# Four instead of eight second-layer value tiles of the first batch element before the next element's values

## The chip, the cores and the metric

The kernel runs on one core of one Trainium2 chip. The metric is the device time in microseconds of one execution, the median over several. A NeuronCore has a matrix engine (TensorE, here PE, with its weight loads as PEld), a vector engine (VectorE, DVE), a scalar engine (ScalarE, ACT), GpSimd (POOL) and SyncE (SP). In this kernel SP issues every transfer between the chip's main memory and the core's on-chip memory; 16 DMA engines carry the bytes out. Each engine executes its own instructions in order and waits for the others by semaphores.

## What is computed

Two layers of a decoder run for one new token of each of four batch elements. A layer is an attention block and a feed-forward block, each behind a layer norm and with a residual addition. Both layers have the same weights and read the same key and value caches. Cut to what matters, the reference is:

```python
x = A_x                                             # 4 x 1 x 512
for layer in range(2):
    h = layernorm(x)
    q = (h @ wq).reshape(B, 1, 32, 128)             # 32 query heads, 8 key/value heads
    p = softmax(q @ k_cache.T * 128 ** -0.5)        # 4096 positions, 4 query heads share a cache head
    x = x + (p @ v_cache).reshape(B, 1, 4096) @ wo
    h = layernorm(x)
    x = x + (gelu(h @ w_gate) * (h @ w_up)) @ w_down
```

The caches are in bfloat16, 4 elements x 8 heads x 4096 positions x 128: 33.5 MB of keys and as much of values. The second layer's attention of an element needs the first layer's complete result for that element, and nothing of the other elements.

## The kernel before

**Tiles.** The eight cache heads are two groups of four (`GH = 4`). Each head's cache is two tiles of 512 KB (`NT = 2`, 128 partitions x 16 positions x 128), so an element has 16 key tiles and 16 value tiles. The key tiles have 16 fixed buffers (`KT`), enough for one element. Value tiles go through seven buffers (`KV_BUFS = 7`).

**Order over elements.** Call the first and second layer's attention of element b F(b) and S(b). Keys are loaded once per element: they are transposed in place on DVE (`Keys.turn`, line 372), used for F(b), and stay until S(b) has used them; only then may the next element's keys overwrite them. Values are too large to stay, so they are loaded twice, once for F(b), once for S(b). Two tiles of element 0 (`KEEP = 2`) are kept from F(0) for S(0) and are loaded once. A value tile below is named by its use: F1-0 to F1-15 are the tiles of F(1) in order of use, S0-0 to S0-15 those of S(0).

One stage, `attend(b2, b1)`, does the scores of S(b2), lets the keys of element b1 into the key buffers as these become free, turns them, and does F(b1). Then `dense` does the feed-forward block of element b1's first layer, and behind it come the second layer's queries for element b1, after which the next stage can free the key buffers. All the work of S(b2) on values that is not done early in the stage is a filler: `dense` and the lines after it call `fill(n)`, which is `Values.step` of S(b2), at ten places with ten tiles in all, and the next stage calls `rest` for what is left.

**The planned order of values.** One list, `order` (lines 441 to 446), fixes the sequence of all value tiles: F(0), then for each b the first `early[b]` tiles of S(b), all of F(b+1), and the remaining tiles of S(b). `early` is eight for element 0 (`TG`, one head group) and four for the others (`2 * NT`, one head pair). Both loads (`load_v`) and uses (`Values.step`) follow this list, and an assertion holds the uses to it. `load_v` issues the next load as soon as one of the seven buffers is free. A tile's buffer is free once its 16 matmuls (line 481, `ot`) are done. While `seen["hold"]` is set, only second-layer tiles may be loaded.

**Keys against values on SP's queue.** In a stage, four key loads (line 365) follow each of the four score blocks of S(b2), as each block frees four key tiles. For element 0 the last four are left out there and issued after the first four tiles of S(0) were used:

```python
if not (t and early[b2] == TG):          # lines 519 and 520
    keys.load(GH)
...
vals2.step(2 * NT)                        # lines 534 to 538
if early[b2] == TG:
    keys.load(GH)
    seen["hold"] = False
    load_v()
```

In the other stages `hold` is taken off right after the score blocks (lines 521 to 523). The rest of the early tiles of S(b2) is used while keys turn: `early - 5` tiles after the first block of F(b1)'s scores (line 560), and the last one after the softmax of that group has begun (line 566). With `early` of four both of these are empty.

Of the kernel before, what the change touches and what calls it, by code (L numbers as in the profile page):

```python
# [30 lines left out]
def kernel(  # L31
# [14 lines left out]
    B, Sq, D = A_x.shape  # L46
# [9 lines left out]
    NT = C // CH  # L56
# [5 lines left out]
    TG = GH * NT  # L62
# [373 lines left out]
    def value_order(b, last):  # L436
        if not last:
            return [(b, last, g, s, t) for g in groups(b) for s in range(GH) for t in range(NT)]
        return [(b, last, g, s, t) for g in groups(b + 1) for s in (3, 2, 0, 1) for t in range(NT)]

    early = [TG] + [2 * NT] * (B - 2)
    order = value_order(0, 0)
    for b in range(B - 1):
        n = early[b]
# [300 lines left out]
```

## Time and profile before

| | |
|---|---|
| median of 6 runs | 317.67 us (316.12 to 318.26) |
| the profiled execution's own time | 318.18 us |
| its span, first to last instruction | 316.4 us |
| PE, DVE, ACT busy | 213.2, 171.1, 28.9 us |
| bytes read | 113.5 MB, 359 GB/s over the span |
| DMA queue's packets, share of 16 engines' span | 93.8% |
| value loads | 118 into value buffers, 8 into freed key buffers at the end, 512 KB each |
| key loads | 64 of 512 KB |

The profile gives, for one execution, the busy time of each engine, the granted clock of PE, the bytes that the DMA engines moved in each slice or in a chosen window, the order in time of each engine's instructions with the wait before each, and the chain of work that ended last, traced back from the end. "SPq" is the issue of a transfer by SP; its landing is the arrival of the last byte. A busy DMA engine isn't always one at its best rate, so the GB/s of a window says more than the busy share. "Turn" below is the DVE transposition of a key tile, 1214 ns each on the mean.

### The profile page before, as it was taken

To read this page: it belongs to the slowest core of one execution; us is meant where nothing else is said; L and a number is where in the kernel's file an instruction comes from. 1 tells how busy PE (TensorE), PEld (TensorE's weight loads), DVE (VectorE), ACT (ScalarE), POOL (GpSimd) and SP (SyncE) were. 2 spreads that over 40 slices of the span, in tenths; PEclk is the share of its full clock that TensorE was granted. 3 is DMA by queue.
4 is the path that set the end of the run, shared out by engine and by line. 5 is a ranking of instruction groups with operands and counts; after the bars stand their busy time and mean duration, and the time that the engine had idled before them with its cause. 6 is when DMAs were issued, how large, how long until landed. Compare 5 with 4: busy or idle time off the path is not lost.

```text
span 316.4 us, 8713 instructions
## 1 busy us (share of the span) xinstructions
PE 213.2 (67%) x3844; PEld 122.3 (39%) x3844; DVE 171.1 (54%) x481; ACT 28.9 (9%) x70; POOL 0.7 (0%) x6
## 2 busy tenths in 40 slices
PE   1460585343576826989876589899762897998875
PEld 0010244121324314556342246564411464645654
DVE  5575751013248875525469874453789543545133
ACT  0002001000002020300020204000202040003100
POOL 0000000000000000000000000000000000000000
PEclk9999999999999555555595555575855555759555
DMA  7999999999939999999999999999999999999900
GB/s 256 383 411 388 409 410 404 351 376 388 390 125 356 404 395 410 407 407 390 356 314 411 410 407 393 355 404 407 408 409 409 408 374 339 407 367 409 368 9 3
DMA packets 35526, 114.09 MB, mean 361 GB/s; under 512 B 3224, under 2 KB 9120, under 8 KB 35488
## 3 DMA queue, kind: packets, MB, share of 16 engines
q1 hardware_dynamic: 35488, 113.53, 93.8%
q8 instruction: 30, 0.49, 0.6%
q14 instruction: 8, 0.07, 0.1%
HBM read 113.51 MB, written 0.00 MB: 359 GB/s over the span
## 4 chain that ended last, share of the span: by engine, by line
DMA 50%; PE 23%; DVE 13%; SPq 9%; issue 3%; ACT 1%; DVEq 0%; ACTq 0%
DMA v<-in_A_v_cache_dram 26%; DMA kt<-in_A_k_cache_dram 21%; PE ot L481 6%; PE sc L383 5%; DVE kt L372 4%; DMA wd_sb<-in_B_w_down_dram 3%; SPq L127 3%; PE rows L280 3%; SPq L133 3%; PE rows L314 3%; PE y L347 2%; PE rows L225 2%; PE x L429 1%; DVE pp L410 1%; SPq L128 1%
## 5 line engine op out<-in xcount | busy, mean ns | idle before, releaser
L481 PEld LDWEIGHTS <-v 128*128 128x128 bf16 x1920 | 59.3, 104 | 52.8 <-DMA v<-in_A_v_cache_dram 30.8
L481 PE MATMUL ot<-pe,v 128*128 128x4 bf16 x1920 | 63.2, 166 | 22.3 <-DMA v<-in_A_v_cache_dram 21.0
L372 DVE STREAM_TRANSPOSE kt<-kt 128x1024 f32<-128x1024 f32 x64 | 74.7, 1214 | 4.8 <-DMA kt<-in_A_k_cache_dram 4.8
L383 PE MATMUL sc<-kt,qb 128*32 128x512 bf16 x512 | 64.2, 557 | 15.8 <-DVE kt L372 11.2
L215 DVE STREAM_TRANSPOSE rows<-rows 128x512 f32<-128x512 f32 (+1 forms) x23 | 16.3, 707 | 39.4 <-PE rows L225 20.0
L383 PEld LDWEIGHTS <-qb 128*32 128x32 bf16 x512 | 17.7, 117 | 45.6 <-issue 33.8
L402 ACT ACTIVATE pp<-sc,nm 128x512 bf16<-128x512 f32 x16 | 11.0, 688 | 155.5 <-DVE junk L398 155.4
L489 DVE TENSOR_TENSOR OT_bf<-ot,rden 128x8 bf16<-128x8 f32 (+1 forms) x40 | 6.5, 163 | 34.0 <-PE ot L481 33.5
L429 PE MATMUL x<-pp,ident_bf 128*32 128x128 bf16 x256 | 9.1, 283 | 20.7 <-DVE pp L410 20.6
L280 PE MATMUL rows<-wo_sb,OT_bf 128*1 128x512 bf16 (+1 forms) x136 | 17.2, 611 | 7.3 <-DMA wo_sb<-in_A_wo_dram 6.3
L225 PE MATMUL rows<-wq_sb,xn_bf 128*1 128x512 bf16 (+1 forms) x160 | 18.9, 623 | 4.7 <-DMA wq_sb<-in_A_wq_dram 4.4
L389 DVE TENSOR_REDUCE m<-sc 128x1 f32<-128x512 f32 x16 | 10.8, 675 | 12.5 <-PE sc L383 12.5
L429 PEld LDWEIGHTS <-ident_bf 128*32 128x32 bf16 x256 | 6.6, 121 | 26.4 <-issue 24.6
L410 DVE STREAM_TRANSPOSE pp<-pp 128x512 bf16<-128x512 bf16 x16 | 11.3, 704 | 5.7 <-ACT pp L402 5.4
L432 ACT CAST pe<-x 128x512 bf16<-128x512 f32 x16 | 9.4, 585 | 21.0 <-PE x L429 21.0
L347 PE MATMUL y<-H_bf,wd_sb 128*128 128x1 bf16 (+1 forms) x280 | 8.4, 165 | 3.8 <-DMA wd_sb<-in_B_w_down_dram 3.0
L249 DVE TENSOR_TENSOR qb<-qe,amask 128x256 bf16<-128x256 f32 x16 | 6.8, 425 | 6.2 <-PE qe L246 6.2
L347 PEld LDWEIGHTS <-wd_sb 128*128 128x128 bf16 x280 | 7.9, 101 | 5.2 <-DMA wd_sb<-in_B_w_down_dram 4.0
L225 PEld LDWEIGHTS <-xn_bf 128*1 128x1 bf16 (+1 forms) x160 | 4.6, 111 | 12.8 <-issue 11.5
L246 PE MATMUL qe<-qm,t_bf 128*128 128x64 bf16 x16 | 3.5, 216 | 8.8 <-DVE qm L236 6.7
L415 PE MATMUL den<-zx,mean_f 128*128 128x16 f32 x32 | 8.9, 357 | 0.0
L420 DVE RECIPROCAL rden<-den 128x16 f32<-128x16 f32 x16 | 4.0, 251 | 8.5 <-PE den L415 8.0
(78 smaller groups left out, 124.3 us busy)
## 6 DMA issues: line engine op xcount, KB each, us to landing
v<-in_A_v_cache_dram SPq DMA_DIRECT2D x118, 512.0 KB, 8.7
kt<-in_A_k_cache_dram SPq DMA_DIRECT2D x64, 512.0 KB, 10.4
wq_sb<-in_A_wq_dram SPq DMA_DIRECT2D x2, 2048.0 KB, 7.7
wo_sb<-in_A_wo_dram SPq DMA_DIRECT2D x4, 1024.0 KB, 11.8
kt<-in_A_v_cache_dram SPq DMA_DIRECT2D x8, 512.0 KB, 9.9
wg_sb<-in_B_w_gate_dram SPq DMA_DIRECT2D x1, 1792.0 KB, 13.5
wu_sb<-in_B_w_up_dram SPq DMA_DIRECT2D x1, 1792.0 KB
wd_sb<-in_B_w_down_dram SPq DMA_DIRECT2D x1, 896.0 KB, 16.9
```

The source lines that it names most:

```text
L127: dq.dma_start(out=wo_sb[:, i * n:(i + 1) * n], in_=wo_dram[:, i * n:(i + 1) * n])
L215: nc.vector.transpose(out=rows[:, :n], in_=rows[:, :n])
L225: nc.tensor.matmul(rows[j * QS:j * QS + nb, :], lhsT=xn_bf[:, k, bs], rhs=w, start=(k == 0), stop=(k == KD - 1))
L280: nc.tensor.matmul(rows[r0:r0 + lhsT.shape[-1], :], lhsT=lhsT, rhs=wo_sb[:, i, :], start=(start and n < QD), stop=(stop and n >= hp - QD))
L347: nc.tensor.matmul(y[:, k], lhsT=wd_sb[:, c, k * P:(k + 1) * P], rhs=H_bf[:, c, :], start=(c == 0 and k == 0), stop=(c == KF - 1), skip_gr ...
L372: nc.vector.transpose(out=words, in_=words)
L383: nc.tensor.matmul(sc[s * QS:(s + 1) * QS], lhsT=qb[:, w0:w0 + 2 * W], rhs=kt[:, :, be // 2, :, be % 2], start=(t == 0 and be == 0), stop= ...
L389: nc.vector.tensor_reduce(out=m[:], in_=sc.rearrange("p c j -> p (c j)"), axis=AX.X, op=ALU.max)
L402: nc.scalar.activation(out=pp[:], in_=sc[:], func=ACT.Exp, bias=nm[:, 0:1], scale=scale, accum_out=ls[:])
L410: nc.vector.transpose(out=flat, in_=flat)
L429: nc.tensor.matmul(x[a * QS:(a + 1) * QS, s], lhsT=ident_bf[:, s * QS:(s + 1) * QS], rhs=pT[:, a], start=True, stop=True, skip_group_check ...
L481: nc.tensor.matmul(self.ot[:, s % 2], lhsT=v[:, i, :], rhs=pe[:, s, c, :], start=(c == 0), stop=(c == C - 1), skip_group_check=True)
```

## The change

`early` becomes four for element 0 as for the others. Nothing else in the text changes, but the branches on `early[b2] == TG` now never apply. For element 0, S0-4 to S0-7 move in the planned order from before F(1) to behind it: their loads, their 64 matmuls and weight loads and their two DVE evictions (line 489). The last four key loads of element 1 are issued with the others, after the fourth score block, and `hold` comes off there. S(0) has 12 tiles left for the fillers in place of eight.

```diff
-    early = [TG] + [2 * NT] * (B - 2)
+    early = [2 * NT] * (B - 1)
     order = value_order(0, 0)
     for b in range(B - 1):
         n = early[b]
         order += value_order(b, 1)[:n] + value_order(b + 1, 0) + value_order(b, 1)[n:]
```

## The prediction

> **What bounds the kernel now.** I read the page first, for the DMA share by slices and the chain; then SP's timeline, for the sequence of loads; then PE's timeline, for the waits that put marks on the stages; last the windows between these marks. Of the page:
>
> ```profile
> GB/s 256 383 411 388 409 410 404 351 376 388 390 125 356 404 395 410 407 407 390 356 314 411 410 407 393 355 404 407 408 409 409 408 374 339 407 367 409 368 9 3
> q1 hardware_dynamic: 35488, 113.53, 93.8%
> DMA 50%; PE 23%; DVE 13%; SPq 9%; issue 3%; ACT 1%; DVEq 0%; ACTq 0%
> ```
>
> Transfers end last: half of the chain, and 94% of the engines' span. In good slices 410 GB/s, so a tile of 524,288 bytes takes 1.279 us. The slices below that are what an order can win or lose. One is deep, 125 GB/s at 87 to 95 us (element 0's feed-forward is over, the keys aren't free yet); the ones at 150 to 166 us (356, 314) are the same place for element 1, and milder.
>
> SP's timeline, issues merged by kind:
>
> ```profile
> 75.62 4.13 SPq L461 DMA_DIRECT2D v<-in_A_v_cache_dram  x5
> 91.84 9.50 SPq L365 DMA_DIRECT2D kt<-in_A_k_cache_dram  x12
> 102.17 0.33 SPq L461 DMA_DIRECT2D v<-in_A_v_cache_dram  x1
> 103.40 5.13 SPq L365 DMA_DIRECT2D kt<-in_A_k_cache_dram  x4
> 109.54 44.56 SPq L461 DMA_DIRECT2D v<-in_A_v_cache_dram  x31
> 157.14 15.45 SPq L365 DMA_DIRECT2D kt<-in_A_k_cache_dram  x16
> 173.53 41.81 SPq L461 DMA_DIRECT2D v<-in_A_v_cache_dram  x30
> 217.01 17.57 SPq L365 DMA_DIRECT2D kt<-in_A_k_cache_dram  x16
> ```
>
> By the planned order the five are S0-2 to S0-6 (S0-0 and S0-1 are kept), the single one S0-7, the 31 are F1-0 to F1-15, S0-8 to S0-15, S1-0 to S1-3, F2-0 to F2-2. So element 2's stage, from 157.14, starts with four second-layer and three first-layer tiles in the seven buffers, and the change gives element 1's stage the same: S0-0 to S0-3 and F1-0 to F1-2.
>
> PE's timeline:
>
> ```profile
> 105.92 1.44 PE L481 MATMUL ot<-pe,v 128*128 128x4 bf16 x48
> 113.81 0.59 PE L481 MATMUL ot<-pe,v 128*128 128x4 bf16 x16 [3.25 <-DMA v<-in_A_v_cache_dram]
> 120.20 0.59 PE L481 MATMUL ot<-pe,v 128*128 128x4 bf16 x16 [3.13 <-DMA v<-in_A_v_cache_dram]
> 142.88 0.59 PE L481 MATMUL ot<-pe,v 128*128 128x4 bf16 x16 [0.27 <-DMA v<-in_A_v_cache_dram]
> 180.50 1.01 PE L481 MATMUL ot<-pe,v 128*128 128x4 bf16 x32
> 203.01 0.59 PE L481 MATMUL ot<-pe,v 128*128 128x4 bf16 x16 [0.27 <-DMA v<-in_A_v_cache_dram]
> 268.00 0.59 PE L481 MATMUL ot<-pe,v 128*128 128x4 bf16 x16 [0.25 <-DMA v<-in_A_v_cache_dram]
> ```
>
> The first two rows are S0-4 to S0-6 and S0-7, the uses that move; 120.20 is F1-0, 180.50 F2-0 and F2-1. The rows at 142.88, 203.01 and 268.00 are the second filler tile of each `dense`, right before the gate matmuls, and each waits for its load: marks at which landings set the time. Windows between the marks and the first key loads:
>
> ```profile
> 91.80:142.90 51.10, 36.08 (x662) 21.10 (x651) 31.73 (x66) 6.58 (x16) 0.00 (x0) 0.59 0.99 383
> 150.00:164.00 14.00, 11.24 (x160) 5.00 (x156) 7.54 (x33) 1.09 (x3) 0.00 (x0) 0.66 0.93 319
> 196.00:203.00 7.00, 5.62 (x126) 3.90 (x123) 2.04 (x12) 0.00 (x0) 0.00 (x0) 0.50 1.00 336
> 217.00:228.00 11.00, 9.32 (x182) 5.23 (x175) 6.67 (x16) 1.67 (x4) 0.00 (x0) 0.81 1.02 407
> 254.00:268.00 14.00, 11.39 (x235) 7.82 (x235) 5.23 (x21) 2.77 (x8) 0.00 (x0) 0.50 0.97 351
> ```
>
> Columns: stretch, length, busy PE, PEld, DVE, ACT, POOL, granted clock, DMA share, GB/s. Against 410 GB/s, 150 to 164 loses 14 x (1 - 319/410) = 3.1 us, 196 to 203 1.3 us, 254 to 268 2.0 us; 217 to 228, the keys of element 3, which come behind a stock of value loads, only 0.1 us.
>
> **The change, part by part.** *Loads before element 1's keys.* Still five, since buffers and not the order limit them: S0-2, S0-3, F1-0, F1-1, F1-2. The hole at 87 to 95 us stays as it is: nothing, provided that `hold` isn't yet on when they are issued, and it is not (it comes on in the stage behind).
>
> *Four key loads move on SP's queue ahead of S0-7.* They land one tile, 1.28 us, earlier. DVE turns 16 keys at 1.214 us and has them back to back until about 123 us, so an earlier landing of the last four is worth nothing by itself. Queued behind them on SP are F1-3 onward: no later than now, as one load fewer stands ahead.
>
> *Four tiles and their uses leave the stretch before 142.88.* Transfers: 4 x 1.279 = 5.1 us. PE: 1.44 + 0.59 = 2.0 us of matmuls, and the 3.25 us wait at 113.81, behind which the softmax's transposition on DVE is queued. DVE: two evictions of about 0.17 us. The mark's tile is no longer S0-9 but S0-5, four landings sooner: 142.88 - 5.12 = 137.76. Can PE and DVE follow? Element 2's stage runs the same program from the same buffers: from first key load to mark 203.01 - 157.14 = 45.87 us, with hardly a PE wait for a value ahead of the mark. Laid on 91.84 this is 137.71. Both agree; I take 137.71, a lead of 5.17 us.
>
> *They come back behind the mark.* Between the marks at 142.88 and 203.01 lie 60.13 us and 44 loads (6 of S(0), 4 and then 2 of S(1), 16 keys, 16 of F(2)). With the change it is 48, from S0-5 to S1-5, as now from 203.01 to 268.00: 64.99 us. The four loads thus cost 4.86 and not 5.12 us: the gap of 3.1 us at 150 to 164 closes, because 15 loads in place of 13 cover the 14 us from mark to keys (15 x 1.279 = 19.2 us), but element 3's stage pays almost as much further on (2.0 us at 254 to 268). New mark: 137.71 + 64.99 = 202.70 for 203.01.
>
> *Fillers on PE.* `dense` and the query work behind it have ten fillers in place of eight, two more of 0.59 us. They lie beside DVE's rsqrt and transposition: element 2 has all ten and takes 14.0 us from mark to first key load, element 1 with eight 14.26 us. Nothing. If that cover went, 1.2 us before the keys are freed, still under the stock of loads.
>
> *From there to the end* both kernels do the same: 64.99 us to the next mark and 48.4 us to the end.
>
> Sum: -5.17 + 4.86 = -0.31 us on a span of 316.4 us. The profiled execution took 318.18 us, its span and 1.8 us around it, 0.5 us above the median of 317.67. On the median: **317.4 us**.
>
> Bounds. The first term: 4.0 us, if the dip of 196 to 203 came to element 1's stage on top of what it has now (5.17 less 1.26), to 6.4 us, if element 1 has none, as its 405 GB/s of today would suggest. The second: at least 48 x 1.279 - 60.13 = 1.3 us, with every load at the full rate; at most 5.12 us, if the key gap stayed. Together from -5.1 to +1.1 us. I stay with the two stages measured, as they run the very order that the change brings.
>
> A rule of the Trainium skill would say that nothing can be won: HBM Reference, Specifications (TRN2), puts a core's effective share at about 358 GB/s, and the page's 359 GB/s over the span looks like that limit reached. By it a tile would be an estimated 1.46 us and every reordering worth zero. The same section says that a core streaming alone measures well above its share; the slices of 404 to 411 GB/s here agree with that.
>
> **The rivals.** *A, faster:* the losses of the two stages that I copied are their own accident. For it: element 1 has now 405 GB/s from 98 to 142.9 us, without their dip. Against: both stages with four early tiles show it, at the same place, the last values of F before the mark. Without the 1.3 us of 196 to 203 and half of the 2.0 us: 317.4 - 2.3 = 315.1 us.
>
> *B, slower:* F1-0 to F1-2 sit in buffers through the keys' turning, so behind the 16 keys only four value loads can be issued, and the queue waits for the first use of F(1). In element 2's stage that use (180.50) came in time: the next load, issued at 181.12, landed 7.7 us later, a load on the empty queue (91.84) 4.0 us, so 3.7 us of work were left. If element 1's use came as late as today (120.20, against 180.50 - 65.30 = 115.20), the queue would be dry 5.0 - 3.7 = 1.3 us, and filling it again costs what 91.8 to 98 us shows (224 GB/s, 2.8 us): +4.1 - 0.3, 321.2 us. Against: today's lateness is the wait for F1-0 itself, which has then landed long before. It decides from 3.7 us of delay on.
>
> *C, not given back:* the 5.2 us stay, 312.5 us, if the later loads hid wholly in the gap; against it, that gap holds 3.1 us.
>
> *D, the change does nothing:* excluded, as both `order` and the branches follow `early`.
>
> **How the numbers follow.** My forecast 0.57, A 0.22, B 0.16, C 0.05. About 0.5%, 1.6 us, can be told from no change here. A (mostly) and C give faster 0.26, the forecast same 0.57, B slower 0.17. Range: low end at A, 315.0; the high end, with the forecast's bound of +1.1 (318.8) inside, goes part of the way to B: 319.7.
>
> **What would show it.** SP's groups: 5 values, 16 keys in one group, 30 values, 16 keys, 32 values. Marks near 137.7, 202.7 and 267.7 us; keys of element 2 near 151.7; no slice of 314 GB/s there. The first use of F(1) near 115, without a DMA wait. Wrong if the first mark is later than 139 (B: a thin queue between 112 and 125), or if the second comes earlier than 201 (A). A shift behind the second mark is none of this.

## The result

The changed kernel takes 316.88 us (median of 35 runs, 314.11 to 320.91), the kernel before in the same sessions 317.17 us (72 runs). The ratio is 0.9988, with a 95% interval of 0.9969 to 1.0006: -0.4 us, between -1.0 and +0.2. Some executions of either kernel fall in a slower state of the chip; they are in the medians, but the ratios here and below leave them out. No difference can be told, as forecast (317.4 us, -0.31 us). The two profiled executions differ by more, 313.5 against 316.4 us of span; 1.2 us of that lie ahead of element 1's first key load, where both kernels do the same, so the spans are not compared, only the distances between marks.

### The profile page after: what moved, and what is told of

Its sections match the earlier page's. It is cut to its first block, busy times and chain, and to the rows that moved or that the text cites. A ratio compares the mean times of both kernels' runs of the same rounds, so it can differ in the third digit from the quotient of the medians.

```text
span 313.5 us, 8714 instructions
## 1 busy us (share of the span) xinstructions
PE 212.3 (68%) x3844; PEld 121.8 (39%) x3844; DVE 171.0 (55%) x481; ACT 28.9 (9%) x70; POOL 0.7 (0%) x6
## 4 chain that ended last, share of the span: by engine, by line
DMA 44%; PE 26%; DVE 15%; SPq 9%; issue 3%; ACT 1%; DVEq 0%; ACTq 0%
DMA kt<-in_A_k_cache_dram 22%; DMA v<-in_A_v_cache_dram 19%; PE sc L383 7%; PE ot L481 6%; DVE kt L372 5%; DMA wd_sb<-in_B_w_down_dram 3%; PE rows L314 3%; PE rows L280 3%; SPq L127 3%; SPq L133 3%; PE y L347 2%; PE rows L225 2%; DVE rows L215 1%; DVE qb L249 1%; PE x L429 1%
```

## The profile after

The page of the changed kernel, the three lines that answer to those of before:

```profile
GB/s 249 405 411 391 408 410 405 353 376 389 389 152 353 409 403 407 379 385 408 396 399 410 409 408 385 380 346 341 409 409 409 409 407 348 399 392 377 408 31 3
q1 hardware_dynamic: 35488, 113.53, 94.2%
DMA 44%; PE 26%; DVE 15%; SPq 9%; issue 3%; ACT 1%; DVEq 0%; ACTq 0%
```

The hole ahead of element 1's keys is still there (152), the dip to 314 at 158 to 166 us is gone, and dips to 346 and 341 stand later instead, at 204 to 219 us. The bytes are the same. DMA's share of the chain is smaller, PE's and DVE's larger: a first sign, no more, that the engines' own work may have become the limit somewhere.

SP's timeline and PE's, changed kernel:

```profile
75.34 4.27 SPq L461 DMA_DIRECT2D v<-in_A_v_cache_dram  x5
90.64 15.87 SPq L365 DMA_DIRECT2D kt<-in_A_k_cache_dram  x16
107.45 41.60 SPq L461 DMA_DIRECT2D v<-in_A_v_cache_dram  x30
150.73 16.77 SPq L365 DMA_DIRECT2D kt<-in_A_k_cache_dram  x16
168.41 45.93 SPq L461 DMA_DIRECT2D v<-in_A_v_cache_dram  x32
216.01 16.66 SPq L365 DMA_DIRECT2D kt<-in_A_k_cache_dram  x16
```

```profile
114.15 1.02 PE L481 MATMUL ot<-pe,v 128*128 128x4 bf16 x32
136.76 0.59 PE L481 MATMUL ot<-pe,v 128*128 128x4 bf16 x16 [0.26 <-DMA v<-in_A_v_cache_dram]
178.69 0.59 PE L481 MATMUL ot<-pe,v 128*128 128x4 bf16 x16 [2.95 <-DMA v<-in_A_v_cache_dram]
201.99 0.58 PE L481 MATMUL ot<-pe,v 128*128 128x4 bf16 x16 [1.66 <-DMA v<-in_A_v_cache_dram]
265.99 0.58 PE L481 MATMUL ot<-pe,v 128*128 128x4 bf16 x16 [0.23 <-DMA v<-in_A_v_cache_dram]
```

The groups of loads are 5, 16, 30, 16, 32, as worked out. F1-0 and F1-1 are used at 114.15 without a wait; F2-1, the second tile of F(2), now waits 2.95 us for its load. The marks are 136.76, 201.99 and 265.99. The last windows, with the columns explained in the prediction:

```profile
90.60:136.80 46.20, 35.26 (x598) 19.31 (x587) 31.54 (x65) 6.68 (x16) 0.00 (x0) 0.60 0.98 371
129.70:136.80 7.10, 5.67 (x125) 3.88 (x123) 2.03 (x12) 0.00 (x0) 0.00 (x0) 0.50 1.00 350
136.80:150.70 13.90, 13.18 (x271) 7.73 (x275) 7.93 (x42) 0.21 (x1) 0.00 (x0) 0.62 1.03 407
150.70:202.00 51.30, 35.56 (x629) 20.16 (x619) 32.94 (x73) 6.58 (x16) 0.00 (x0) 0.57 1.02 398
202.00:216.00 14.00, 13.27 (x271) 7.98 (x275) 6.81 (x35) 0.21 (x1) 0.00 (x0) 0.62 0.94 339
```

Element 1's stage has taken over the dip ahead of its mark (350 GB/s), and the gap ahead of element 2's keys is closed (407); one has opened ahead of element 3's (339, where the kernel before had 401 at 203 to 217).

PE's waits for value loads say the same more directly. From the first use of F(1) to the gate matmuls they sum to 5.50 us in the kernel before (3.13 us at 120.20 is the largest) and to 0.26 us after. From the first use of F(2) it is the other way round: 0.27 us before, 6.53 us after (2.95 and 1.66 us in the rows above, and four smaller waits).

For the experiments one measure is used throughout: the time from an element's first key load to its gate matmuls (line 314, `rows<-wg_sb`, right behind the mark), for elements 1, 2 and 3. "Ratio" is always against the kernel before, timed in the same session. The stages are those of one profiled execution per row, and the same kernel profiled twice (after and e10, e2 and e11) differs by up to 1.1 us for elements 1 and 2 and 1.9 us for element 3; a smaller difference within a column says nothing.

| kernel | element 1 | element 2 | element 3 | ratio (95% interval) |
|---|---|---|---|---|
| before | 51.56 | 46.39 | 51.50 | 1 |
| after | 46.64 | 51.77 | 50.49 | 0.9988 (0.9969 to 1.0006) |
| e1, old order, keys together | 52.45 | 48.35 | 51.44 | 1.0068 (1.0034 to 1.0102) |
| e2, new order, keys apart | 46.59 | 50.23 | 51.94 | 1.0035 (0.9999 to 1.0070) |
| e11, as e2 | 46.33 | 49.89 | 50.09 | 1.0001 (0.9963 to 1.0040) |
| e10, as after | 47.72 | 50.63 | 50.77 | 0.9995 (0.9951 to 1.0039) |
| e3, hold set early | 49.16 | 50.35 | 51.43 | 1.0067 (1.0027 to 1.0107) |
| e4, after, no loads of S0-4 to S0-7 | 46.38 | 51.22 | 52.40 | 0.9958 (0.9919 to 0.9997) |
| e5, before, no loads of S0-4 to S0-7 | 46.47 | 46.78 | 51.03 | 0.9877 (0.9838 to 0.9917) |
| e6, after, no loads of F2-4 to F2-7 | 46.62 | 47.55 | 51.26 | 0.9893 (0.9857 to 0.9929) |
| e12, after, no loads of F1-4 to F1-7 | 46.40 | 50.25 | 51.29 | 1.0018 (0.9975 to 1.0061) |
| e7, eight early tiles everywhere | 51.67 | 51.40 | 51.18 | 1.0166 (1.0120 to 1.0212) |
| e8, after, six buffers | 49.47 | 51.51 | 51.49 | 1.0236 (1.0187 to 1.0285) |
| e9, before, six buffers | 53.98 | 48.83 | 51.55 | 1.0318 (1.0269 to 1.0368) |

The change does one thing in this table that stands clear of this: the short stage moves from element 2 to element 1. The experiments ask why a stage is short, and what makes it long.

## Experiments: the two parts of the change

**e1: the keys' part alone.** The old order of values, with element 1's last four key loads ahead of S0-7.

```diff
-                if not (t and early[b2] == TG):
-                    keys.load(GH)
+                keys.load(GH)
...
             if early[b2] == TG:
-                keys.load(GH)
                 seen["hold"] = False
```

> One part of the change alone: the order of values stays as before (eight early tiles of S(0)), but element 1's last four key loads are issued with the others, ahead of S0-7. Theory (the time is set by transport, and the bytes are the same): S0-7 lands four tiles later, near 119 us in place of 113.8, and PE waits some 8 us for it with the softmax's transposition queued behind; the first use of F(1) comes about 2 us later than 120.2, but the DMA queue has F1-0 to F1-5 to load meanwhile and doesn't run dry, so the mark at 142.9 moves by 0 to 2 us and the whole by 0 to +1 us. Rival (what PE and DVE wait for in this stage is the price, and the change removed it): the longer wait is paid in full, +5 us.

PE's timeline of e1:

```profile
117.57 0.58 PE L481 MATMUL ot<-pe,v 128*128 128x4 bf16 x16 [7.66 <-DMA v<-in_A_v_cache_dram]
```

The wait is the one expected (7.66 us for 8), and F(1) is first used at 120.64, 29.7 us after the first key load in place of 28.4. The time is 2.2 us longer (0.34% to 1.02%), between the two expectations and above the theory's. The longer wait is mostly absorbed: in the profile only 0.9 us of it is in element 1's stage. Another 2.0 us are in element 2's (48.35 for 46.39), whose order of loads is that of the kernel before; why, no run shows. So the old branch, which kept four key loads behind S0-7, was worth something with eight early tiles.

**e2 and e11: the values' part alone.** The new order, with the last four key loads and the end of `hold` still after the first four uses of S(0).

```diff
-                if not (t and early[b2] == TG):
+                if not (t and b2 == 0):
...
-            if early[b2] < TG:
+            if b2 > 0:
...
-            if early[b2] == TG:
+            if b2 == 0:
```

> The other part alone: four early tiles of S(0) as in the changed kernel, but element 1's last four key loads still wait until these four tiles are used, and hold comes off only there. Theory: the four tiles are used within 2 us of the last score block, and the queue is full then, so the keys go out no later than it takes them: the same as the changed kernel, 316.9 us within 0.5 us. Rival (the keys' earlier issue is what pays for the tiles parked in buffers): 1 us or more slower than the changed kernel.

The stages showed nothing (46.59 us for element 1, against 46.64), but the median was 1.2 us above the kernel before's in that session. So it was run again next to the changed kernel.

> The changed kernel once more, unchanged, as the partner of e11. Theory: 0.9988 of the kernel before within 0.35%.

> The kernel of e2 once more beside the changed kernel on one chip: four early tiles, the last four key loads of element 1 after their use. Theory: the stage's marks are those of the changed kernel, so the two medians agree within 0.4%. Rival (the e2 timing was no accident): this one is again 0.4% or more slower than the changed kernel.

Side by side the ratios are 0.9995 (e10) and 1.0001 (e11). With four early tiles it doesn't matter when the last four keys are issued, as far as the 0.4% on either side of each ratio can tell; the first timing of e2, which lay outside what its theory allowed, did not come again. What the change does is done by its order of values.

**e3: the five loads ahead of the keys.** `hold` is set before element 0's weights are loaded, so only S0-2 and S0-3 are loaded ahead of element 1's keys.

```diff
             seen["upto"] = len(loads)
+            seen["hold"] = True
             load_v()
```

> The changed kernel with hold set already when element 0's feed-forward weights are loaded, so that F1-0 to F1-2 aren't loaded into the three buffers ahead of element 1's keys but after them. Theory: three tiles of 1.279 us are taken out of a stretch in which the queue runs empty anyway and must be loaded later: +3.8 us, all of it visible as a hole before element 1's keys. Rival B of the prediction (first-layer tiles that sit in buffers while keys turn starve the queue behind the keys): the three free buffers give back 1 to 3 us of it, +1 to +3 us.

Against the changed kernel it is 0.8% or 2.5 us slower, 1.0067 over 0.9988, and element 1's stage is 2.5 us longer (49.16 for 46.64). That is less than the 3.8 us of three tiles. That could be the rival's buffers giving something back. The next experiments suggest another reason: the changed kernel's stage hardly waits for values, so it had room for about one more load (3.8 - 2.5 = 1.3 us). With the three loads behind the keys PE waits 4.94 us for values in this stage. Neither reason was separated from the other.

## Experiments: what four loads are worth, and where

These leave out 2 MB of loads at one place. The matmuls stay, with a part of `wo_sb` for the missing tiles.

```diff
+    moved = value_order(0, 1)[4:8]
-    loads = [u for u in order if not (u[1] and (u[0],) + u[2:] in keep)]
+    loads = [u for u in order if not (u[1] and (u[0],) + u[2:] in keep) and u not in moved]
...
-                v = held[b, g, s, t]
+                v = wo_sb[:, CH:2 * CH, :Dh] if use in moved else held[b, g, s, t]
...
-                if last or (b, g, s, t) not in keep:
+                if use not in moved and (last or (b, g, s, t) not in keep):
```

**e4: the four moved tiles, at their new place**, in the changed kernel.

> The changed kernel without the four loads of S0-4 to S0-7: their matmuls read a part of wo_sb in place of the value tiles, so the second-layer output of four heads' part is left out. Theory: transport is the currency, four tiles are worth 5.1 us wherever they stand: about 311.8 us, the second mark 5.1 us earlier against the first key load. Rival C of the prediction turned round (the loads behind the mark are hidden in the gap before the next keys): less than 2 us.

Here the theory of the prediction fell. Its 5.1 us are 1.0 us against the changed kernel (0.9958 over 0.9988), with an interval of about 1.4 us to either side when those of the two ratios are put together, so not told from nothing. SP's timeline and the windows of e4:

```profile
107.79 41.17 SPq L462 DMA_DIRECT2D v<-in_A_v_cache_dram  x26
150.53 17.41 SPq L365 DMA_DIRECT2D kt<-in_A_k_cache_dram  x16
```

```profile
136.80:150.50 13.70, 12.98 (x268) 7.76 (x269) 8.06 (x43) 0.21 (x1) 0.00 (x0) 0.62 0.79 266
150.50:201.20 50.70, 35.55 (x629) 20.19 (x617) 32.12 (x66) 6.58 (x16) 0.00 (x0) 0.57 1.01 386
```

Four loads fewer are issued between the keys (26 for 30), and the queue idles instead: 266 GB/s for 13.7 us, a loss of 13.7 x (1 - 266/410) = 4.8 us. The keys of element 2 go out when the dense work and the query are done, 13.5 us behind the gate matmuls with the loads or without. Loads at that place are filling. And the stage that follows stays long, 51.22 us, with the same wait for F2-1 (2.95 us at 179.11): it wasn't these four loads that made it so.

**e5: the same four tiles at their old place**, in the kernel before. The edit is the same.

> The kernel before without the four loads of S0-4 to S0-7, at their old place ahead of element 1's mark; their matmuls read a part of wo_sb, so that part of the second layer's output is wrong in value and the time is that of a kernel which leaves 2 MB of reading out. Theory now (a stage has two floors: its own work, 46.4 us from the first key load to the gate matmuls as elements 1 and 2 showed it, and its transport; ahead of the mark of element 1 the transport is the higher one): element 1's stage falls from 51.5 to 46.4 to 47.5 us, the later ones stay as before, so -4 to -5 us in all. Rival (the four loads are worth little here too, as e4 found behind the mark): less than 1.5 us.

SP's and PE's timelines of e5, first key loads and gate matmuls of elements 1 and 2:

```profile
91.09 15.72 SPq L365 DMA_DIRECT2D kt<-in_A_k_cache_dram  x16
151.31 15.52 SPq L365 DMA_DIRECT2D kt<-in_A_k_cache_dram  x16
```

```profile
137.56 1.66 PE L314 MATMUL rows<-wg_sb,xn_bf 128*1 128x448 bf16 x16
198.09 1.66 PE L314 MATMUL rows<-wg_sb,xn_bf 128*1 128x448 bf16 x16
```

137.56 - 91.09 = 46.47 us, 198.09 - 151.31 = 46.78 us: two short stages, and the whole is 1.23% or 3.9 us faster (2.6 to 5.1), at the lower edge of what was expected. At the old place the four loads were worth that; at the new one 1.0 us, not told from nothing.

**e6 and e12: four loads of F(2), four of F(1), in the changed kernel**, each ahead of its element's mark. Only the first line of the edit differs: `value_order(2, 0)[4:8]` and `value_order(1, 0)[4:8]`.

> The changed kernel without the loads of F2-4 to F2-7, the same number of bytes as in e4 but between element 2's keys and its mark; their matmuls read a part of wo_sb, so the first layer's output of element 2 is wrong in value. Theory now (loads ahead of the mark are on the path, the ones behind it fill the 14 us of dense work): element 2's stage falls from 51.8 to between 46.4 and 48 us, -4 to -5 us in all, although e4's same four loads brought under 2 us. Rival (the stage is held by its own work once the fillers are ten): less than 1.5 us.

> The changed kernel without the loads of F1-4 to F1-7, four loads between element 1's keys and its mark, where e5 took four out of the kernel before; their matmuls read a part of wo_sb, so the first layer's output of element 1 is wrong in value. Theory now (a stage takes the larger of its own work, 46.4 us from first key load to gate matmuls, and its transport; in the changed kernel element 1's stage is at its own work): element 1's stage stays at 46.3 to 46.7 us, element 2's at 50 to 52 us, and the whole within 1 us of the changed kernel. Rival (every load ahead of a mark is on the path, whatever the stage's work): -4 to -5 us, as in e5 and e6.

e6, element 2's first key load and its gate matmuls, then e12, element 1's, with the mark between them:

```profile
151.23 16.37 SPq L365 DMA_DIRECT2D kt<-in_A_k_cache_dram  x16
198.78 1.66 PE L314 MATMUL rows<-wg_sb,xn_bf 128*1 128x448 bf16 x16
```

```profile
90.82 15.65 SPq L365 DMA_DIRECT2D kt<-in_A_k_cache_dram  x16
136.72 0.57 PE L482 MATMUL ot<-pe,v 128*128 128x4 bf16 x16
137.22 1.66 PE L314 MATMUL rows<-wg_sb,xn_bf 128*1 128x448 bf16 x16
```

```profile
91.00:137.00 46.00, 35.37 (x604) 19.50 (x597) 31.23 (x64) 6.69 (x16) 0.00 (x0) 0.61 0.88 331
```

In element 2's stage, the long one, four loads are worth 3.0 us (0.9893 over 0.9988, about 1.3 us to either side), less than the 4 to 5 expected; the stage takes 47.55 us for 51.77. In element 1's, the short one, they are worth nothing that can be told: the whole is 0.3% slower, within noise, the stage takes 46.40 us for 46.64, and DMA just moves less, 331 GB/s for 371. Four loads ahead of the same mark were worth 3.9 us in the kernel before (e5).

A stage has two floors: its own work, some 46.4 us from first key load to gate matmuls, and its transport. The first is what the stage takes when PE waits for no value load at all: 46.38 us in e4, 46.40 in e12, 46.47 in e5 and 46.59 in e2, all of element 1. In e12 the mark has no wait any more (136.72). Which engine's work sets these 46.4 us, no run here shows. Only where transport is the higher floor is a load on the path.

## Experiments: the opposite change, and one buffer fewer

**e7: eight early tiles for every element.**

```diff
-    early = [TG] + [2 * NT] * (B - 2)
+    early = [TG] * (B - 1)
```

> Eight early second-layer tiles for every element, the change's opposite carried through. Theory now: the elements' stages from first key load to gate matmuls are 51.5, 51.5 and 51.5 us (each now has four loads more ahead of its mark, up to the transport's floor), and the end, with four tiles fewer left behind the last mark, is 4 to 5 us shorter: the same as before within 1 us. Rival A of the prediction (the dips to 330 to 350 GB/s ahead of the marks belong to stages with four early tiles): no dip below 390 GB/s in the 7 us ahead of any mark, and 2 to 3 us faster than before.

The stages came out as expected, 51.67, 51.40 and 51.18 us: none is short. But the end was to be 4 to 5 us shorter, and from the last element's gate matmuls to the store of the output it took 44.67 us, as in the changed kernel (44.70) and 0.9 us less than before (45.58); kernels with the end of the kernel before lie between 44.5 and 45.8 us, so even this is within noise. So the kernel is 1.66% slower, and my count of the end was wrong: four loads fewer behind the last mark buy next to nothing, as behind element 1's. The windows of the 7 us ahead of the gate matmuls in e7:

```profile
135.50:142.50 7.00, 5.83 (x134) 4.21 (x134) 1.87 (x10) 0.00 (x0) 0.00 (x0) 0.50 1.02 401
200.60:207.60 7.00, 5.83 (x141) 4.23 (x137) 2.05 (x12) 0.00 (x0) 0.00 (x0) 0.50 1.03 404
265.50:272.50 7.00, 5.83 (x140) 4.22 (x137) 2.00 (x12) 0.00 (x0) 0.00 (x0) 0.50 1.02 404
```

There is no dip, at 401 to 404 GB/s. That goes with rival A's reading that the dips belong to stages with four early tiles, but not with what it made of them: a kernel without them isn't faster. And e5, with eight early tiles of which four aren't loaded, has 360 GB/s at 129.7 to 136.8 us, so the early tiles alone don't make the dip.

**e8 and e9: `KV_BUFS = 6`, in the changed kernel and in the kernel before.**

> The changed kernel with six value buffers in place of seven. Theory now (from first key load to the gate matmuls a stage takes the larger of 46.4 us and its loads at 1.279 us each plus about 4 us; where its own work is the larger, the tiles lie in their buffers and the queue behind them thins): one load fewer goes into the hole ahead of element 1's keys and one fewer is ready at each later start of keys, and the dips ahead of the marks get deeper: +1 to +2 us in each of the three stages, +3 to +6 us against the changed kernel. Rival B of the prediction (it is the changed order that lives on parked tiles): this kernel loses at least 2 us more by the sixth buffer than the kernel before does.

> The kernel before with six value buffers. Theory now: element 1's stage, where transport is the larger, gets one load more after the hole, +1.3 us, and the others as in the changed kernel: +3 to +6 us, within 1.5 us of the changed kernel's loss. Rival B: at least 2 us less than the changed kernel's loss.

The changed kernel loses 2.5% by the sixth buffer (1.0236 over 0.9988), 7.9 us, the kernel before 3.2%, 10.1 us. Both losses are larger than the 3 to 6 us expected, and they differ by more than the 1.5 us allowed. In the profiles element 1's first key load comes 2.7 us later in e8 than in the changed kernel, 0.3 us later in e9 than in the kernel before; most of the rest is in element 1's stage (e8) or in those of elements 1 and 2 (e9). Rival B had the sign wrong: with less room the changed order is the better one, by 2.3 to 2.6 us of four executions each, which is little more than the noise of such a difference (some 2 us).

## Why the prediction was right

**The number** came from two stages that already ran the new order, and they carried over. The lead: from first key load to element 1's mark 45.87 us forecast, 136.76 - 90.64 = 46.12 measured. The return: from mark to mark 64.99 forecast, 201.99 - 136.76 = 65.23 measured. From first key load to the second mark before took 203.01 - 91.84 = 111.17 us, after 201.99 - 90.64 = 111.35: +0.18 for the -0.31 of the sum, less than a median here can tell. That the single terms agree to 0.25 us is luck: in the second profile of the changed kernel (e10) element 1's stage is 1.1 us longer and element 2's 1.1 us shorter.

**Loads before element 1's keys**: five, as said, and the hole stayed (152 GB/s in its slice). **The four key loads on SP's queue**: worth nothing by themselves, as e11 beside e10 showed within 0.4%. **Fillers**: from mark to element 2's keys 13.97 us with ten, forecast 14.0.

**The reason given for the lead was half of it.** I took 5.17 us as four transports of 1.279 us and asked only whether PE and DVE could follow. They can just barely: the stage then stands on its own work (e12), and that 5.1 us of transport less end just at the 46.4 us of work is chance. The bound of 6.4 us for this term could not have been reached; no stage in any run is under 46.3 us. "Marks at which landings set the time" was also more than the rows say: element 2's mark in the kernel before waits only 0.27 us for its load, and PE waits for no other value in that stage.

**The reason given for the return was wrong.** "The four loads thus cost 4.86 and not 5.12 us" puts the return down to the moved tiles' transport. e4 took that transport away, and element 2's stage stayed at 51.22 us. What goes with the longer stage is the place in the list at which element 2's keys begin. Of the 12 late tiles of S(0) only ten are fillers ahead of the keys, the last two are used in the next stage, when `hold` is on. So at the keys' first issue 37 value tiles from S0-0 on have been loaded or are on their way (30 used, seven buffers), up to F2-0; before it were 39 (32 used), up to F2-2. F2-1 and F2-2 now come behind the keys. The traces show it: F2-1 is waited for 2.95 us (178.69), where F2-0 and F2-1 were used without a wait before (180.50), and the same wait, 2.5 to 3.0 us, stands in e2, e3, e4, e10, e11 and e12, in e6 with 2.65.

The other runs bear it out. By SP's groups three tiles of F(2) are ahead of element 2's keys in the kernel before, e1 and e5, and its stage takes 46.39, 48.35 and 46.78 us; two in e9, 48.83; one in the changed kernel and in e2, e3, e4, e10, e11 and e12, 49.89 to 51.77; none in e7 (which has four more early tiles of S(1) instead) and e8, 51.40 and 51.51. No run moves this place and nothing else, so the cause is read from the waits and from this row, not isolated. That loads ahead of the mark are on the path in this stage is shown by e6; that the four moved ones, behind element 1's mark, weren't worth their transport, by e4.

**Slips that change nothing.** S0-4 to S0-7 have one DVE eviction (114.43 us in the kernel before), not two. DVE's turns weren't back to back until 123 us: between those at 111.90 and 115.14 DVE waited 1.30 us for the product of S0-7. The lower bound of the first term is 5.17 - 1.26 = 3.9, not 4.0 (so +1.2 for +1.1 of both together), and B's sum takes the 0.3 us off twice (317.4 + 4.1 = 321.5).

**The rivals.** A: a dip came along to element 1's stage (350 GB/s at 129.7 to 136.8), so it wasn't an accident, and the -2.3 us didn't come. B: F(1)'s first use at 114.15 us is 23.5 us behind the first key load (28.4 before), without a wait, and e8 and e9 show no sign of it. C: nothing of the 5.2 us stayed.

**The rule of the Trainium skill** (HBM Reference, Specifications (TRN2)) that a core's effective share is about 358 GB/s is no limit here: e7's windows ahead of the gate matmuls ran at 401 to 404 GB/s. Nor is every reordering worth zero: e7 reads the same 113.5 MB as the kernel before and is 1.66% slower. The 2 MB that e5 leaves out would be an estimated 5.9 us by that rule and are 5.1 us at 410 GB/s; the 3.9 us measured don't decide between the two, as its stage meets the floor of its own work.

## What to carry to other kernels

Two parts of a kernel that already run the order which a change brings to a third forecast it well here, though the reasons given for its terms were half wrong; the condition is that they start from the same state of buffers. A transport is worth its time only in a stage where it is the higher of two floors: leave the bytes of a few loads out at one place at a time, and the kernel tells which stage that is. A high DMA share over the whole span doesn't tell it: here it was 94% in both kernels, and four loads were worth 3.9 us, 3.0 us, or at two places nothing that could be told from noise.

## What was unexpected in the hardware

A DMA share near 1 stood beside very different rates with tiles of one size: 403 GB/s at share 1.02 (98 to 129.7 us of the changed kernel), 350 at 1.00 (129.7 to 136.8). What makes the low ones, no run here shows. The medians of the kernel before lie between 316.3 and 317.3 us from one session to the next, on three chips, which is as much as the smallest effects asked for here; so each kernel enters here by its ratio to the one timed beside it.
